# Attention ahead of two layers of experts: scores and exponentials issued by head, with the two row halves out of step

## The chip, the cores and the metric

One core of one Trainium2 chip runs the whole program in one launch. The metric is the device time of that launch in microseconds (us); lower is better. The engines are named as in the profile: PE (TensorE matmul) with PEld (its weight loads), DVE (VectorE), ACT (ScalarE), POOL (GpSimd), SP (SyncE, which here only issues DMAs).

## The reference

Three stages follow one another in float32: attention with pooled queries, a mixture of 4 experts for every token, and a mixture of 8 experts with one expert per token. The change touches the first stage and where it hands over to the second.

```python
batch, n_heads, seq, head_dim = 2, 8, 1152, 64
q_pool = q.reshape(B, H, S // 2, 2, D).mean(axis=3)             # 576 query rows
scores = scale * np.matmul(q_pool, k.transpose(0, 1, 3, 2))     # 576 x 1152
scores = scores - np.max(scores, axis=-1, keepdims=True)
attn = np.exp(scores)
attn = attn / (np.sum(attn, axis=-1, keepdims=True) + 1e-09)
attn_out = np.matmul(attn, v)
# x: attn_out as 1152 x 512; then
# moe1: out += p[:, e] * (relu(x @ w1[e]) @ w2[e]) for 4 experts, 512 -> 1024 -> 512
# moe2: the same with 8 experts, of which each row takes one
```

## The kernel before

The 16 (batch, head) combinations go through in 8 pairs of heads. The first head of a pair lies on partitions 0 to 63, the second on 64 to 127, so that a matmul of one head uses one half of TensorE's rows and the two heads' matmuls can run side by side. A pair has two jobs, g = 2p with 256 query rows and g = 2p + 1 with 320, and a job has 9 chunks of 128 keys. A job is issued in two halves: the first takes chunks 0 to 3, the second chunks 4 to 8. Scores are kept transposed, keys on partitions and query rows along the free axis.

For one chunk, `score` (L105 to L113) issues four matmuls for each head into one PSUM tile S of two banks: high part of q with high and low part of k, low part of q with high part of k, and a row of ones with the negated row maximum, mr. One ACT instruction (L113) then takes the exponential of both heads, 128 x 512 or 128 x 640, into a tile E. There are two S tiles, so the scores of chunk c + 2 wait until the exponential of chunk c has read its tile. POOL adds the E tiles of a job up (`add`, L120), eight additions a job. PE multiplies E by v into O (`av`, L126) and sums the added tile over the keys with a matrix of ones (`total`, L132). ACT copies the sums (L134) and O (L138), DVE takes reciprocals (L140), POOL multiplies (L142), ACT casts the high part of x and POOL takes the low part (L149, L150). The last job differs: `ndir` gives it four chunks that PE sums itself (eight matmuls with ones) in place of POOL.

The row maxima of the next job are made among the scores of this one: `smax` (L80 to L86) issues one 384-key matmul for each head and DVE reduces each; the last 64 rows of both heads go together in `tmax` (L90, L91). `mT` (L101 to L104) turns the maxima into mr. The first half of a shorter job also transposes q of the next pair (L69), the last half of a longer job k of the pair after that (L58), with ACT making the high parts and DVE the low parts. The order of the instructions on each engine is the order in which this code is written out by hand, since the scheduler is off for the stretch.

After attention, weights go in 128 x 1024 pieces through a staging tile `st` (DMA on SP, L204), a cast to the high part on ACT (L212) and a subtraction for the low part on DVE (L215), into a tile w of a ring. Staging and ring are allocated in the room that attention's pools leave when they close. The pool `ld`, which holds the k and q as loaded, lies on the right side, and `kq`, which holds their parts, on the left; the first four ring tiles thus lie under `ld`, which is free once the last pair has been transposed, and the first four splits stand inside the last pairs.

Loads of the first pair are issued on SP (k) and on ACT's queue (q), those of the second pair on ACT's queue (L39 to L42), all later ones on SP.

Of the kernel before, what the change touches and what calls it, by code (L numbers as in the profile page):

```python
# [9 lines left out]
def attention(tc, q, k, v, xT, identF, NJ=16):  # L10

    nc=tc.nc
    B,H,S,D=q.shape
    Q=S//2; NC=S//128; NP=NJ//2; NG=2*NP; C1=4
    DI=0
    RB=(0,); RA=(1,2)
    JOB=((0,256),(256,320))
    HD=(slice(0,64),slice(64,128))
    with ExitStack() as ctx:
        def pool(name,bufs,**kw): return ctx.enter_context(tc.tile_pool(name=name,bufs=bufs,**kw))  # L20
        ld=pool("ld",2,side="right")
        one=pool("one",1); vp=pool("vp",3); ep=pool("ep",10); es=pool("es",2); fp=pool("fp",3); sm=pool("sm",3); kq=pool("kq",2)
# [9 lines left out]
        def load(p):  # L32
            b,h0=divmod(2*p,H)
            kn=ld.tile([128,NC,2,D],F32,name="kn"); qn=ld.tile([128,2,5,2,D],F32,name="qn"); vn=vp.tile([128,2,NC,D],F32,name="vn")
            st['ld',p]=kn,qn; st['v',p]=vn
            ek,eq=(nc.sync,nc.scalar) if p==0 else (nc.scalar,nc.scalar) if p==1 else (nc.sync,nc.sync)
            ks=[slice(0,3),slice(3,6),slice(6,9)] if p==0 else [slice(0,9)]
            for n in range(2):
                eq.dma_start(qn[:,n,0:4],q[b,h0+n,0:1024].rearrange("(i p r) d -> p i r d",p=128,r=2))  # L39
                eq.dma_start(qn[:,n,4],q[b,h0+n,896:1152].rearrange("(p r) d -> p r d",r=2))  # L40
            for c in ks:
                for n in range(2): ek.dma_start(kn[:,c,n],k[b,h0+n].rearrange("(p c) d -> p c d",c=NC)[:,c])  # L42
            if p>1: load_v(p)
# [9 lines left out]
        def kT(p,g):  # L53
            if g==0: st['k',p]=[kq.tile([128,S],F32R,name=n) for n in ("kh","kl")]
            kn=st['ld',p][0]; kh,kl=st['k',p]
            f=T1(384) if g<2 or p==0 else psS.tile([128,2,512],F32,name="S")[:,0,0:384]
            cs=slice(g*384,(g+1)*384)
            for m in range(3): nc.tensor.transpose(f[:,m*128:(m+1)*128],kn[:,3*g+m].rearrange("p h d -> p (h d)"),identF)  # L58
            nc.scalar.copy(kh[:,cs],f)
            lo=lambda: nc.vector.tensor_tensor(out=kl[:,cs],in0=f,in1=kh[:,cs].bitcast(F32),op=ALU.subtract)  # L60
            if p==0: st['lo',g]=lo
            else: lo()
        def qT(p):
            st['q',p]=[kq.tile([128,Q],F32R,name=n) for n in ("qh","ql")]
            qs=st['qs',p]; qh,ql=st['q',p]
            if p==0: s0=psS.tile([128,2,512],F32,name="S")
            for mm,o,cs in ((range(4),0,slice(0,512)),((4,),64,slice(512,576))):
                f=T1(512) if p else (s0[:,0] if o==0 else s0[:,1])
                for i,m in enumerate(mm): nc.tensor.transpose(f[:,i*128:(i+1)*128],qs[:,m].rearrange("p h d -> p (h d)"),identF)  # L69
                src=f[:,o:o+cs.stop-cs.start]  # L70
                nc.scalar.activation(out=qh[:,cs],in_=src,func=AF.Copy,scale=0.0625)
                nc.vector.scalar_tensor_tensor(out=ql[:,cs],in0=src,scalar=0.0625,in1=qh[:,cs].bitcast(F32),op0=ALU.mult,op1=ALU.subtract)
            for h in range(2): nc.gpsimd.tensor_copy(qt[p%2][HD[h],HD[h]],qh[HD[h],512:576])
# [3 lines left out]
        def smax(g,i,early=False):  # L77

            p,u=divmod(g,2); c,t=divmod(i,2); m=m3(g); kh=st['k',p][0]; qh=st['q',p][0]
            if early: ss=psS.tile([128,2,512],F32,name="S")[:,:,0:384].rearrange("p h n -> h p n")  # L80
            else: ss=[T1(384) for h in range(2)]
            for h in range(2):
                nc.tensor.matmul(ss[h],qh[HD[h],(2*u+t)*128:(2*u+t+1)*128],kh[HD[h],c*384:(c+1)*384],start=True,stop=True)  # L83
            if early: nc.vector.tensor_reduce(out=m[:,t,:,c],in_=ss.rearrange("h p n -> p h n"),axis=AX.X,op=ALU.max)
            else:
                for h in range(2): nc.vector.tensor_reduce(out=m[:,t,h,c:c+1],in_=ss[h],axis=AX.X,op=ALU.max)  # L86
# [18 lines left out]
        def score(g,c):  # L105
            p,u=divmod(g,2); o,n=JOB[u]
            kh,kl=st['k',p]; qh,ql=st['q',p]; mr=st['m',g]
            s=psS.tile([128,2,512],F32,name="S"); cs=slice(c*128,(c+1)*128); os=slice(o,o+n)
            ops=((kh[:,cs],qh[:,os]),(kl[:,cs],qh[:,os]),(kh[:,cs],ql[:,os]),(ones,mr))
            for i,(l,r) in enumerate(ops):  # L110
                for h in range(2): nc.tensor.matmul(s[:,h,0:n],l[HD[h]],r[HD[h]],start=i==0,stop=i==3)  # L111
            E=ep.tile([128,2,320],F32,name="E"); st['E',g,c]=E
            nc.scalar.activation(out=E[:,:,0:n],in_=s[:,:,0:n],func=AF.Exp)  # L113
        def ndir(g): return 4 if g==NG-1 else DI
# [38 lines left out]
        with tc.manual_schedule():  # L153
            qsum(0)
            for n in range(3): kT(0,n)
            qT(0)
            load_v(0)
            for i in range(6): smax(0,i,True)
            neg(0); st['lo',0](); mT(0); st['lo',1](); st['lo',2]()
            load(1); load_v(1)  # L160
            for h in range(4*NP):
# [7 lines left out]
                for i,c in enumerate(range(C1) if first else range(C1,NC)):  # L169
                    if rl and i in RB: smax(*rl.pop(0))  # L170
                    score(g,c)
                    add(g,c)
                    if rl and i in RA: smax(*rl.pop(0))
                    if h==0:
                        for _ in range(2):
                            if rl: smax(*rl.pop(0))
                    if first and c==2 and g>1: fin(g-2)
# [606 lines left out]
```

## Time and profile before

| | us |
|---|---|
| runs shown | 818.16 to 824.17, median 822.31 of 3 |
| the profiled execution | 819.94, of which the span is 818.1 |
| attention ends, experts begin | 257.21 |
| PE busy | 783.2 (96%) |
| DVE / ACT / POOL busy | 374.1 / 300.9 / 278.1 |

The profile follows one execution. Its span runs from the first to the last instruction; the device time holds 1.8 us more. In the 40 slices of the page POOL stands at 9 for slices 4 to 12, the slices of attention, PE at 9 nearly everywhere, and the granted TensorE clock at 9 of 10 or more in every slice. Times of rows are us from the span's start; in the trace's names S is the score tile, T a shared PSUM tile, m and M the maxima, es the sum of exponentials.

### The profile page before, as it was taken

The page shows a single profiled execution, that of the slowest core. Times are in us where ns is not written, and L with a number is a line of the kernel's source. Part 1 is how long each engine was busy: PE and PEld are TensorE (multiplying, and loading weights), DVE is VectorE, ACT ScalarE, POOL GpSimd, SP SyncE. Part 2 cuts the span into 40 slices and gives each one's busy share as a digit, 9 for nine tenths or more (in the row PEclk, how much of TensorE's full clock was granted, in tenths as well). Part 3 has the DMA queues.
Part 4 walks back from the last instruction along what each step waited for, and adds up shares of the span by engine and source line. Part 5 has one row for each costly group of instructions (what it writes and reads, how often), then busy time and mean ns, then how long its engine had stood idle before and what let it go on. Part 6 is the DMA issues. An engine that isn't in the chain of part 4 may idle for free. (4 is left out here: it accounts for less than half of the span.)

```text
span 818.1 us, 13046 instructions
## 1 busy us (share of the span) xinstructions
PE 783.2 (96%) x5128; PEld 641.0 (78%) x5128; DVE 374.1 (46%) x789; ACT 300.9 (37%) x557; POOL 278.1 (34%) x256
## 2 busy tenths in 40 slices
PE   4999999998999999999999999999999999998996
PEld 2667677666667998998989989889898888877673
DVE  4676867777836110431214412144253589563510
ACT  1356555556546121330103301033141455471611
POOL 1689999999994000000000000000000242442301
PEclk9999999999999999999999999999999999999998
DMA  8703311301206000140003100000053141996981
GB/s 280 180 2 91 91 53 40 91 31 32 74 1 229 6 1 1 61 145 1 1 1 102 54 0 1 1 1 1 26 183 153 40 168 46 339 333 234 335 295 70
DMA packets 57735, 77.53 MB, mean 95 GB/s; under 512 B 23031, under 2 KB 33271, under 8 KB 57664
## 3 DMA queue, kind: packets, MB, share of 16 engines
q1 hardware_dynamic: 50752, 69.12, 25.3%
q0 software_dynamic: 1600, 4.98, 1.8%
q10 hardware_dynamic: 5312, 2.49, 1.2%
q8 instruction: 43, 0.70, 0.4%
q14 instruction: 28, 0.23, 0.1%
HBM read 71.86 MB, written 4.98 MB: 94 GB/s over the span
## 5 line engine op out<-in xcount | busy, mean ns | idle before, releaser
L120 POOL TENSOR_TENSOR es<-es,E 128x512 f32<-128x512 f32 (+1 forms) x108 | 154.3, 1429 | 7.7 <-ACT E L113 0.9
L375 POOL TENSOR_TENSOR r_n<-r_ss,half 128x1 f32<-128x1 f32 x9 | 5.8, 649 | 372.7 <-ACT X L374 372.6
L245 PE MATMUL ps<-xb,w 128*128 128x384 f32 x384 | 129.4, 337 | 0.0
L243 PE MATMUL ps<-xb,w 128*128 128x384 f32 x384 | 129.3, 337 | 0.0
L248 DVE SCALAR_TENSOR_TENSOR hl<-ps,hh 128x384 fp32r<-128x384 f32 x96 | 53.4, 557 | 150.3 <-ACT hh L247 150.1
L247 ACT ACTIVATE hh<-ps 128x384 fp32r<-128x384 f32 x96 | 47.2, 491 | 201.0 <-PE ps L245 201.0
L113 ACT ACTIVATE E<-S 128x512 f32<-128x512 f32 (+1 forms) x144 | 90.0, 650 | 72.8 <-PE S L111 65.6
L258 PE MATMUL py<-w,hl 128*128 128x512 f32 x288 | 113.4, 394 | 0.0
L257 PE MATMUL py<-w,hh 128*128 128x512 f32 x288 | 113.1, 393 | 0.0
L256 PE MATMUL py<-w,hh 128*128 128x512 f32 x288 | 112.5, 391 | 0.0
L86 DVE TENSOR_REDUCE m<-T 128x1 f32<-128x384 f32 x180 | 91.5, 552 | 32.1 <-PE T L83 29.3
L244 PE MATMUL ps<-xc,w 128*128 128x384 f32 x288 | 97.0, 337 | 0.0
L215 DVE TENSOR_TENSOR w<-st,w 128x1024 fp32r<-128x1024 f32 x53 | 74.5, 1419 | 42.4 <-ACT w L212 41.1
L126 PE MATMUL O<-E,vn 128*64 128x320 f32 (+1 forms) x576 | 76.9, 411 | 0.0
L212 ACT CAST w<-st 128x1024 fp32r<-128x1024 f32 x60 | 61.8, 1054 | 36.2 <-PE py L258 23.9
L243 PEld LDWEIGHTS ps<-xb,w 128*128 128x128 f32 x384 | 72.1, 188 | 0.9 <-issue 0.5
L245 PEld LDWEIGHTS ps<-xb,w 128*128 128x128 f32 x384 | 72.1, 188 | 0.0
L257 PEld LDWEIGHTS py<-w,hh 128*128 128x128 f32 x288 | 54.1, 188 | 11.7
L256 PEld LDWEIGHTS py<-w,hh 128*128 128x128 f32 x288 | 54.1, 188 | 11.3
L258 PEld LDWEIGHTS py<-w,hl 128*128 128x128 f32 x288 | 54.1, 188 | 10.9
L262 DVE SCALAR_TENSOR_TENSOR y<-py,p,y 128x512 f32<-128x512 f32 x27 | 20.2, 750 | 90.6 <-PE py L258 90.6
L126 PEld LDWEIGHTS O<-E,vn 128*64 128x64 f32 x576 | 38.6, 136 | 28.1 <-issue 5.5
(369 smaller groups left out, 1342.4 us busy)
## 6 DMA issues: line engine op xcount, KB each, us to landing
st<-in_moe_w SPq DMA_DIRECT2D x104, 512.0 KB, 5.5
vn<-in_v SPq DMA_DIRECT2D x14, 288.0 KB, 3.4
kn<-in_k SPq DMA_DIRECT2D x12, 288.0 KB
qn<-in_q SPq DMA_DIRECT2D x12, 256.0 KB, 4.2
ysc<-y SPq DMA_DIRECT2D x9, 256.0 KB, 2.0
qn<-in_q ACTq DMA_DIRECT2D x4, 256.0 KB, 3.8
qn<-in_q SPq DMA_DIRECT2D x12, 64.0 KB, 3.7
kn<-in_k SPq DMA_DIRECT2D x6, 96.0 KB, 3.6
```

The costliest lines, as they stand in the source:

```text
L86: for h in range(2): nc.vector.tensor_reduce(out=m[:,t,h,c:c+1],in_=ss[h],axis=AX.X,op=ALU.max)
L113: nc.scalar.activation(out=E[:,:,0:n],in_=s[:,:,0:n],func=AF.Exp)
L120: nc.gpsimd.tensor_tensor(out=s,in0=st['E',g,0][:,:,0:n] if c==1 else s,in1=st['E',g,c][:,:,0:n],op=ALU.add)
L126: for h in range(2): nc.tensor.matmul(O[HD[h],0:n],vn[:,h,c],st['E',g,c][:,h,0:n],start=c==0,stop=c==NC-1)
L212: if he=='A': nc.scalar.copy(wh,st)
L215: (nc.vector if le=='V' else nc.gpsimd).tensor_tensor(out=wl,in0=st,in1=wh.bitcast(F32),op=ALU.subtract)
L243: nc.tensor.matmul(ps,wh[:,fs],xh[dc],start=(dc==0),stop=False)
L244: nc.tensor.matmul(ps,wh[:,fs],xl[dc],start=False,stop=False)
L245: nc.tensor.matmul(ps,wl[:,fs],xh[dc],start=False,stop=(dc==3))
L256: nc.tensor.matmul(py,hh[:,us],wh[:,cs],start=(fc==0),stop=False)
L257: nc.tensor.matmul(py,hh[:,us],wl[:,cs],start=False,stop=False)
L258: nc.tensor.matmul(py,hl[:,us],wh[:,cs],start=False,stop=(fc==7))
```

## The change

Each head gets its own score tiles, S0 and S1, of one bank each (two of each), and its own exponentials of 256 or 320 columns. `streams` lists the score matmuls and the row maxima of each head by a pattern (S a chunk's scores, m a row maximum), gives each a nominal start, and issues the two heads' lists merged by that; the row maxima of the two heads stand at different places of the patterns. `add` is called when a chunk's second exponential has been issued. In the longer jobs PE sums the last chunk in place of POOL (`ndir`). The small casts of q for the wide maximum move from POOL to ACT. For the first pair, ACT copies the transposed q and k out of PSUM and POOL takes the low parts, where DVE read PSUM. The loads of the second pair are issued on SP right behind the first pair's, and the first maxima stand between the transposes. `ld` and `kq` change sides, so the first ring tiles lie under the parts of k and q, which are read until the last score.

```diff
-    DI=0
-    RB=(0,); RA=(1,2)
+    PAT=(("SSmSmSm","mSSmSmS"),("SSmSmSmS","mSSmSmSS"),("SmmSmmSmmS","SmmSmmSmmS"))
...
-        ld=pool("ld",2,side="right")
-        one=pool("one",1); vp=pool("vp",3); ep=pool("ep",10); es=pool("es",2); fp=pool("fp",3); sm=pool("sm",3); kq=pool("kq",2)
+        ld=pool("ld",2)
+        one=pool("one",1); vp=pool("vp",3); ep=pool("ep",10); es=pool("es",2); fp=pool("fp",3); sm=pool("sm",3); kq=pool("kq",2,side="right")
...
-            ek,eq=(nc.sync,nc.scalar) if p==0 else (nc.scalar,nc.scalar) if p==1 else (nc.sync,nc.sync)
+            ek,eq=(nc.sync,nc.scalar) if p==0 else (nc.sync,nc.sync)
...
-            lo=lambda: nc.vector.tensor_tensor(out=kl[:,cs],in0=f,in1=kh[:,cs].bitcast(F32),op=ALU.subtract)
-            if p==0: st['lo',g]=lo
-            else: lo()
+            if p==0:
+                w=ep.tile([128,2,320],F32,name="E").rearrange("p h n -> p (h n)")[:,0:384]
+                def low():
+                    nc.scalar.copy(w,f)
+                    nc.gpsimd.tensor_tensor(out=kl[:,cs],in0=w,in1=kh[:,cs].bitcast(F32),op=ALU.subtract)
+                st['low',g]=low
+            else: nc.vector.tensor_tensor(out=kl[:,cs],in0=f,in1=kh[:,cs].bitcast(F32),op=ALU.subtract)
...
-            for h in range(2): nc.gpsimd.tensor_copy(qt[p%2][HD[h],HD[h]],qh[HD[h],512:576])
+                if p:
+                    nc.vector.scalar_tensor_tensor(out=ql[:,cs],in0=src,scalar=0.0625,in1=qh[:,cs].bitcast(F32),op0=ALU.mult,op1=ALU.subtract)
+                else:
+                    w=ep.tile([128,2,320],F32,name="E").rearrange("p h n -> p (h n)")[:,0:cs.stop-cs.start]
+                    nc.scalar.activation(out=w,in_=src,func=AF.Copy,scale=0.0625)
+                    nc.gpsimd.tensor_tensor(out=ql[:,cs],in0=w,in1=qh[:,cs].bitcast(F32),op=ALU.subtract)
+            for h in range(2): nc.scalar.copy(qt[p%2][HD[h],HD[h]],qh[HD[h],512:576])
...
+        def smax1(g,i,h,early=False):
+            p,u=divmod(g,2); c,t=divmod(i,2); m=m3(g); kh=st['k',p][0]; qh=st['q',p][0]
+            s=psS.tile([128,512],F32,name=f"S{h}")[:,0:384] if early else T1(384)
+            nc.tensor.matmul(s,qh[HD[h],(2*u+t)*128:(2*u+t+1)*128],kh[HD[h],c*384:(c+1)*384],start=True,stop=True)
+            nc.vector.tensor_reduce(out=m[:,t,h,c:c+1],in_=s,axis=AX.X,op=ALU.max)
         def smax(g,i,early=False):
-            p,u=divmod(g,2); c,t=divmod(i,2); m=m3(g); kh=st['k',p][0]; qh=st['q',p][0]
-            if early: ss=psS.tile([128,2,512],F32,name="S")[:,:,0:384].rearrange("p h n -> h p n")
-            else: ss=[T1(384) for h in range(2)]
-            for h in range(2):
-                nc.tensor.matmul(ss[h],qh[HD[h],(2*u+t)*128:(2*u+t+1)*128],kh[HD[h],c*384:(c+1)*384],start=True,stop=True)
-            if early: nc.vector.tensor_reduce(out=m[:,t,:,c],in_=ss.rearrange("h p n -> p h n"),axis=AX.X,op=ALU.max)
-            else:
-                for h in range(2): nc.vector.tensor_reduce(out=m[:,t,h,c:c+1],in_=ss[h],axis=AX.X,op=ALU.max)
+            for h in range(2): smax1(g,i,h,early)
...
-        def score(g,c):
-            p,u=divmod(g,2); o,n=JOB[u]
-            kh,kl=st['k',p]; qh,ql=st['q',p]; mr=st['m',g]
-            s=psS.tile([128,2,512],F32,name="S"); cs=slice(c*128,(c+1)*128); os=slice(o,o+n)
-            ops=((kh[:,cs],qh[:,os]),(kl[:,cs],qh[:,os]),(kh[:,cs],ql[:,os]),(ones,mr))
-            for i,(l,r) in enumerate(ops):
-                for h in range(2): nc.tensor.matmul(s[:,h,0:n],l[HD[h]],r[HD[h]],start=i==0,stop=i==3)
-            E=ep.tile([128,2,320],F32,name="E"); st['E',g,c]=E
-            nc.scalar.activation(out=E[:,:,0:n],in_=s[:,:,0:n],func=AF.Exp)
-        def ndir(g): return 4 if g==NG-1 else DI
+        def score(g,c,h,i):
+            p,u=divmod(g,2); o,n=JOB[u]; hd=HD[h]
+            kh,kl=st['k',p]; qh,ql=st['q',p]; cs=slice(c*128,(c+1)*128); os=slice(o,o+n)
+            if i==0: st['s',h]=psS.tile([128,512],F32,name=f"S{h}")[:,0:n]
+            s=st['s',h]
+            l,r=((kh[:,cs],qh[:,os]),(kl[:,cs],qh[:,os]),(kh[:,cs],ql[:,os]),(ones,st['m',g]))[i]
+            nc.tensor.matmul(s,l[hd],r[hd],start=i==0,stop=i==3)
+            if i<3: return
+            if ('E',g,c) not in st: st['E',g,c]=ep.tile([128,2,320],F32,name="E"); st['n',g,c]=0
+            nc.scalar.activation(out=st['E',g,c][:,h,0:n],in_=s,func=AF.Exp)
+            st['n',g,c]+=1
+            if st['n',g,c]==2: add(g,c)
+        def streams(g,cs,ms,pat,between):
+            n=JOB[g%2][1]; L=[]
+            for h in range(2):
+                t=0; ci=iter(cs); mi=iter(ms)
+                for x in pat[h]:
+                    if x=='S':
+                        c=next(ci,None)
+                        if c is None: continue
+                        for i in range(4): L.append((t,h,lambda c=c,h=h,i=i: score(g,c,h,i),(c,h,i))); t+=9+.425*n
+                    else:
+                        m=next(mi,None)
+                        if m is None: continue
+                        L.append((t,h,lambda m=m,h=h: smax1(*m,h),None)); t+=172
+            for t,h,f,k in sorted(L,key=lambda z: z[:2]):
+                f()
+                if k: between(*k)
+        def ndir(g): return 4 if g==NG-1 else g%2
...
-            for n in range(3): kT(0,n)
-            qT(0)
+            load(1)
+            kT(0,0); kT(0,1); st['low',0](); qT(0)
+            smax(0,0,True); smax(0,1,True); st['low',1]()
+            kT(0,2); st['low',2]()
+            for i in range(2,6): smax(0,i,True)
             load_v(0)
-            for i in range(6): smax(0,i,True)
-            neg(0); st['lo',0](); mT(0); st['lo',1](); st['lo',2]()
-            load(1); load_v(1)
+            neg(0); mT(0)
+            load_v(1)
...
-                for i,c in enumerate(range(C1) if first else range(C1,NC)):
-                    if rl and i in RB: smax(*rl.pop(0))
-                    score(g,c)
-                    add(g,c)
-                    if rl and i in RA: smax(*rl.pop(0))
-                    if h==0:
-                        for _ in range(2):
-                            if rl: smax(*rl.pop(0))
-                    if first and c==2 and g>1: fin(g-2)
+                def between(c,hh,i):
+                    if hh==1 and i==3 and first and c==2 and g>1: fin(g-2)
+                streams(g,range(C1) if first else range(C1,NC),rl,PAT[h==0 and 2 or (not first)],between)
```

The first place is ACT at the start of the program; qh, kh are high parts, vn, kn, qn loads, E stands in for a scratch copy where it is written from T. Before:

```order
L59 CAST kh<-T 128x384 x3
L71 ACTIVATE qh<-S 128x512
L71 ACTIVATE qh<-S 128x64
L46 DMA vn<-in_v 128x576 x2
L102 CAST mr_222<-T 128x256
L39 DMA qn<-in_q 128x4x128
L40 DMA qn<-in_q 128x128
L39 DMA qn<-in_q 128x4x128
L40 DMA qn<-in_q 128x128
L42 DMA kn<-in_k 128x9x64 x2
L113 ACTIVATE E<-S 128x2x256 x4
```

And with the change:

```order
L58 CAST kh<-T 128x384 x2
L62 COPY E<-T 128x384
L73 ACTIVATE qh<-T 128x512
L78 ACTIVATE E<-T 128x512
L73 ACTIVATE qh<-T 128x64
L78 ACTIVATE E<-T 128x64
L80 COPY qt_138<-qh 64x64 x2
L62 COPY E<-T 128x384
L45 DMA vn<-in_v 128x576 x2
L107 CAST mr_256<-T 128x256
L120 ACTIVATE E<-S_266 128x256
L120 ACTIVATE E<-S_268 128x256
```

The six loads of the second pair have left the place ahead of the first exponential; copies out of PSUM and the two small casts have come in ahead of mr. (One cast and one copy more, of the last third of k, stand ahead of the loads of v.)

The second place is PE in the first half of the shorter job of a late pair; S_2614 and S_2628 are score tiles of the first head, S_2620 and S_2633 of the second, L83 and L88 row maxima. Before:

```order
L83 MATMUL T<-kh,qh 128x384 x2
L111 MATMUL S<-qh,kh 128x256 x2
L111 MATMUL S<-qh,kl 128x256 x2
L111 MATMUL S<-ql,kh 128x256 x2
L111 MATMUL S<-mr_2796,ones 128x256 x2
```

And with the change:

```order
L117 MATMUL S_2614<-qh,kh 128x256
L88 MATMUL T<-kh,qh 128x384
L117 MATMUL S_2614<-qh,kl 128x256
L117 MATMUL S_2620<-qh,kh 128x256
L117 MATMUL S_2614<-ql,kh 128x256
L117 MATMUL S_2620<-qh,kl 128x256
L117 MATMUL S_2614<-mr_2574,ones 128x256
L117 MATMUL S_2620<-ql,kh 128x256
L117 MATMUL S_2628<-qh,kh 128x256
L117 MATMUL S_2620<-mr_2574,ones 128x256
```

Where both heads took the same step together, the first head begins with scores while the second has its row maximum, and the second head follows one step behind; their tiles are filled, and released to the exponentials, one after the other.

The third place is DVE at the end of attention. Before, four low parts of weights (L215) stand among the maxima of the last pairs, of which this is the first piece:

```order
L86 TENSOR_REDUCE m_2610<-T 128x1 x2
L215 TENSOR_TENSOR w<-st,w 128x1024
L86 TENSOR_REDUCE m_2610<-T 128x1 x2
L215 TENSOR_TENSOR w<-st,w 128x1024
L86 TENSOR_REDUCE m_2610<-T 128x1 x2
L215 TENSOR_TENSOR w<-st,w 128x1024
```

With the change the first low parts (L237) stand at the last reciprocals:

```order
L166 RECIPROCAL r<-r 128x128 x2
L237 TENSOR_TENSOR w<-st,w 128x1024 x2
L166 RECIPROCAL r<-r 128x160 x2
L341 TENSOR_SCALAR enT<-X,rt_3920 128x32
L168 TENSOR_TENSOR x<-x,r 128x320
L366 MEMSET base 128x8
L237 TENSOR_TENSOR w<-st,w 128x1024 x2
L176 TENSOR_TENSOR xc_96<-x,xb_95 128x320
```

None is left among the maxima; two go ahead of the last job's reciprocals and two behind its product.

## Rows read from the trace of the kernel before

**Rows 1.** Windows: stretch, length, busy of PE PEld DVE ACT POOL, clock, DMA.

```profile
118.87:147.09 28.22, 27.67 (x273) 19.78 (x272) 20.15 (x39) 16.33 (x35) 27.22 (x25) 1.00 0.26 67
...
175.41:206.80 31.39, 28.40 (x272) 20.00 (x273) 25.20 (x43) 19.87 (x39) 30.39 (x26) 1.00 0.18 55
206.80:233.51 26.71, 25.91 (x257) 18.17 (x256) 18.75 (x35) 14.12 (x29) 25.79 (x23) 1.00 0.11 40
233.51:257.21 23.70, 22.39 (x213) 14.79 (x211) 7.24 (x7) 14.61 (x28) 19.29 (x17) 1.00 0.26 85
```

**Rows 2.** Timeline of POOL: start, duration, engine, line, operation, out<-in, count.

```profile
115.28 1.27 POOL L120 TENSOR_TENSOR es<-E 128x512 f32<-128x512 f32 x1
...
119.79 0.52 POOL L73 CAST qt<-qh 64x64 fp32r<-64x64 f32 x2
...
133.66 9.76 POOL L120 TENSOR_TENSOR es<-es,E 128x640 f32<-128x640 f32 x6
...
144.04 1.29 POOL L120 TENSOR_TENSOR es<-E 128x512 f32<-128x512 f32 x1
```

**Rows 3.** Timeline of PE in a second half of the shorter job.

```profile
118.87 0.28 PE L111 MATMUL S<-qh,kh 64*128 64x256 f32 x2
...
119.34 0.28 PE L111 MATMUL S<-qh,kh 64*128 64x256 f32 x2
...
120.83 0.41 PE L83 MATMUL T<-kh,qh 64*128 64x384 f32 x2
121.00 0.35 PE L111 MATMUL S<-qh,kh 64*128 64x256 f32 x2
...
121.74 0.39 PE L111 MATMUL S<-qh,kh 64*128 64x256 f32 x2
```

**Rows 4.** Groups by shape, ACT, 33.77 to 233.51: busy, mean ns | idle, releasers.

```profile
L113 ACT ACTIVATE E<-S 128x640 f32<-128x640 f32 x63 | 42.9, 704 | 31.0 <-PE S L111 30.1 <-POOL es L120 0.5
L113 ACT ACTIVATE E<-S 128x512 f32<-128x512 f32 x63 | 36.0, 598 | 30.4 <-PE S L111 29.9
```

**Rows 5.** Timeline of ACT: two exponentials in a row.

```profile
113.01 1.09 ACT L113 ACTIVATE E<-S 128x512 f32<-128x512 f32 x2 [2.92 <-PE S L111]
```

**Rows 6.** Waits, 33.77 to 233.51: who waits for what, us in total, times, longest.

```profile
PEld S L111 <- ACT E L113: 16.0, 41, 1.1
...
ACT xb L149 <- POOL x L142: 11.0, 10, 2.4
```

**Rows 7.** Timeline of PE in the last halves.

```profile
247.04 0.41 PE L111 MATMUL S<-qh,kh 64*128 64x320 f32 x2 [0.27 <-ACT E L113]
...
248.75 0.41 PE L111 MATMUL S<-qh,kh 64*128 64x320 f32 x2 [0.27 <-ACT E L113]
...
252.27 2.32 PE L132 MATMUL T<-E,ones 128*64 128x320 f32 x16
```

**Rows 8.** Timeline of DVE in the pair of 31.39 us.

```profile
201.20 1.64 DVE L215 TENSOR_TENSOR w<-st,w 128x1024 fp32r<-128x1024 f32 x1
```

**Rows 9.** Timeline of PE where the heads once ran half a chunk apart.

```profile
206.93 0.28 PE L111 MATMUL S<-qh,kh 64*128 64x256 f32 x1
207.04 0.28 PE L111 MATMUL S<-ql,kh 64*128 64x256 f32 x1
207.05 0.28 PE L111 MATMUL S<-qh,kl 64*128 64x256 f32 x1
```

**Rows 10.** Timeline of ACT and DVE in the first pair.

```profile
25.79 1.09 ACT L113 ACTIVATE E<-S 128x512 f32<-128x512 f32 x2 [5.83 <-DMA qn<-in_q]
...
29.17 1.49 DVE L91 TENSOR_REDUCE m<-T 128x1 f32<-128x384 f32 x3 [2.46 <-PE T L90]
```

**Rows 11.** Timeline of DVE and PE at the hand-over to the experts.

```profile
256.60 1.23 DVE L215 TENSOR_TENSOR w<-st,w 128x1024 fp32r<-128x1024 f32 x1 [1.21 <-ACT w L212]
...
257.74 2.16 DVE L140 RECIPROCAL r<-r 128x160 f32<-128x160 f32 x2
...
264.68 0.41 PE L318 MATMUL X<-identF,en 8*128 8x8 f32 x4 [0.78 <-DVE en L315]
```

More of the change, by code (lines that the diff above doesn't have):

```diff
@@ L55, in kT @@
             kn=st['ld',p][0]; kh,kl=st['k',p]
-            f=T1(384) if g<2 or p==0 else psS.tile([128,2,512],F32,name="S")[:,0,0:384]
+            f=T1(384) if g<2 or p==0 else psS.tile([128,512],F32,name="S0")[:,0:384]
             cs=slice(g*384,(g+1)*384)
@@ L59, in kT @@
             nc.scalar.copy(kh[:,cs],f)
-            lo=lambda: nc.vector.tensor_tensor(out=kl[:,cs],in0=f,in1=kh[:,cs].bitcast(F32),op=ALU.subtract)
-            if p==0: st['lo',g]=lo
-            else: lo()
+            if p==0:
[5 more added lines that the diff above has]
+            else: nc.vector.tensor_tensor(out=kl[:,cs],in0=f,in1=kh[:,cs].bitcast(F32),op=ALU.subtract)
         def qT(p):
             st['q',p]=[kq.tile([128,Q],F32R,name=n) for n in ("qh","ql")]
-            qs=st['qs',p]; qh,ql=st['q',p]
-            if p==0: s0=psS.tile([128,2,512],F32,name="S")
+            qs=st['qs',p]; qh,ql=st['q',p]; ff=[]
             for mm,o,cs in ((range(4),0,slice(0,512)),((4,),64,slice(512,576))):
-                f=T1(512) if p else (s0[:,0] if o==0 else s0[:,1])
+                f=T1(512); ff.append((f[:,o:o+cs.stop-cs.start],cs))
                 for i,m in enumerate(mm): nc.tensor.transpose(f[:,i*128:(i+1)*128],qs[:,m].rearrange("p h d -> p (h d)"),identF)
-                src=f[:,o:o+cs.stop-cs.start]
+            for src,cs in ff:
                 nc.scalar.activation(out=qh[:,cs],in_=src,func=AF.Copy,scale=0.0625)
-                nc.vector.scalar_tensor_tensor(out=ql[:,cs],in0=src,scalar=0.0625,in1=qh[:,cs].bitcast(F32),op0=ALU.mult,op1=ALU.subtract)
-            for h in range(2): nc.gpsimd.tensor_copy(qt[p%2][HD[h],HD[h]],qh[HD[h],512:576])
+                if p:
[5 more added lines that the diff above has]
+            for h in range(2): nc.scalar.copy(qt[p%2][HD[h],HD[h]],qh[HD[h],512:576])
         def m3(g):
```

## The prediction

> **What bounds the kernel now.** The windows come first [rows 1]. Attention ends at 257.21 us; the experts follow. The change edits attention and, of the experts, only the start, so everything behind that is taken to shift unchanged. Within attention a pair of heads takes 28.22 us in the steady middle; PE is busy for 27.67 of it, POOL for 27.22 and ACT for 16.33. Both PE and POOL look full, so the next question is which one the other waits for.
>
> POOL's timeline [rows 2] shows additions back to back. From a pair's first addition to the next pair's is 144.04 - 115.28 = 28.76 us, a little more than PE's pitch: POOL falls behind slowly and would soon be the pace. PE's timeline [rows 3] shows that PE is not full of work. Two chunks start 0.47 apart when nothing holds them, and a pair of row maxima takes 121.00 - 120.83 = 0.17. The five chunks of this half start within 121.74 - 118.87 = 2.87 us, while the work between those starts is 4 x 0.47 + 2 x 0.17 = 2.22: 0.65 us are waits that the modelled matmul ends hide. The four halves of a pair, counted alike, give about 2.0 us (the waits of [rows 6], 16.0 in seven pairs, come to 2.3 each). The waits name the cause [rows 6]: a score weight load stood 41 times, 16.0 us in seven pairs, behind an exponential that had not yet emptied its PSUM tile. So it is the round trip score, exponential, next score that costs, with two tiles to alternate; ACT as a whole is far from full.
>
> **The change, part by part**, against the profiled execution's own 819.94 us. The median of the runs is 822.31, 2.4 higher; I add that at the end.
>
> *Exponentials by head.* ACT takes 0.598 for 512 columns and 0.704 for 640 [rows 4]: 0.83 ns a column and about 0.17 fixed. The second of two in a row adds only 1.09 - 0.60 = 0.49 [rows 5], so about 0.11 of the fixed part hides. By these rows 256 columns cost 0.385 alone and 0.28 in a row, 320 columns 0.44 and 0.33. Two heads need 0.56 or 0.66 of ACT per chunk against 0.47 (0.59 in the longer job) plus maxima on PE. What a score waits for is the exponential of its own head, 0.21 shorter than the joint one, and the heads' halves are moved apart so that ACT takes them in turn. PE's cycle of two chunks, 1.38 to 1.66 us by the starts in [rows 3], gets some 0.2 shorter, and the work in it is 1.1. Of the 2.0 us about 1.35 should go. The rest, 0.65, stays: about 0.15 because ACT's 0.56 exceeds PE's 0.47 where no maximum lies between, and about 0.5 for two low-part casts on ACT, which wait 11.0 us over seven pairs for POOL's product [rows 6] with exponentials queued behind them. Bounds: all 2.0 goes, or nothing.
>
> The Trainium skill, "ScalarE: Activation LUTs", section "What ACT_TABLE_LOAD costs", prices an ACTIVATE with immediate operands at 186 ns plus 0.833 ns a column, with about 93 ns hidden back to back. Here [rows 4] show 0.17 for its fixed part and [rows 5] 0.11 for what hides. By the page, an estimate, a chunk takes ACT 0.61 and 0.72 instead of 0.56 and 0.66; if half of that extra were bare, some 0.5 us a pair, the time would come out 3 to 4 us later. The rows of this case are taken.
>
> *Row maxima and scores in streams.* The number of matmuls is the same; only their order changes. That two row halves run side by side although half a chunk apart is seen once in this trace [rows 9]: one head's third score matmul starts at 207.04 between the other head's first and second, at 206.93 and 207.05, which keep the usual step of 0.12 (a quarter of 0.47). So the new order is costed at nothing, covered by that concurrency; what it costs if that fails is the slower rival below.
>
> *Sum of the last chunk on PE in the longer jobs.* Four rows more on PE per pair: 2.32 for 16 [rows 7] is 0.145 each, so +0.55 (0.58 by that row, 0.5 if the other row half hides some). POOL loses one 640-column addition, 9.76 / 6 = 1.63, and its two casts of 0.52, which go to ACT [rows 2]: its pair becomes 28.76 - 1.63 - 0.52 = 26.6.
>
> *A pair* is then 28.22 - 1.35 + 0.55 = 27.4 on PE, above POOL's 26.6, which stops being the pace. Of the seven pairs from 33.77 to 233.51, six take 27.4 and the last, which has no successor to prepare, 26.71 - 0.8 = 25.9: 190.3 against 199.74, **-9.4**. About 4.0 of that is the pair of 31.39 [rows 1]. There the first weight splits ran on ACT and DVE within the scores, beside POOL's additions, and a low part took 1.64 [rows 8] where one takes 1.23 at 256.60 [rows 11]. With the weights under k and q these splits can only come after the last score, so the pair becomes a normal one.
>
> *The last three halves*, 233.51 to 257.21, have no maxima to cover waits. Two chunks take 248.75 - 247.04 = 1.71 [rows 7] for 1.18 of work, five such waits in all: 2.65. ACT's 0.66 and 0.56 leave 14 chunks with 0.07 to 0.09 each, 1.0. **-1.6** (bounds 0 and -2.6).
>
> *The start.* The first exponential waited 5.83 us behind loads of the second pair that stand on ACT's queue [rows 10]; those are now on SP, issued at the top. The scores could run at about 20 us. The next limit is DVE: 12 maxima and 3 wide ones at 1.49 / 3 = 0.5 are 7.4 us and end near 27.3, where they end at 30.66 now. With the same tail the pairs start 3.3 earlier: **-3.3**. Bounds -1 (the k and q casts of the second pair, or the added ACT copies of the first, are late) and -5 (all that the wait was).
>
> *The hand-over.* Four splits, formerly inside the pairs, now stand between the last exponential and the experts, 1.23 each on DVE [rows 11]. Two low parts go ahead of the last reciprocals there, two behind the product that follows them. The sums end near 255 [rows 7], the reciprocals (2.16) at 257.5 or so, the product must wait for the copy of O after PE's last matmul at 257.2, so I estimate the third low part at 260.5 and the fourth at 261.8 on the present clock. PE, from 257.2 on with three groups in turn at some 0.17 a matmul, comes to them about 0.1 and 0.4 us earlier. The loads that follow wait for those tiles and are wanted some 10 us later: hidden. Against this stands the 0.78 that PE now waits for the router's embedding at 264.68, and which moves. Net **+0.5**; bounds -0.8 (nothing waits) and +3 (two splits and their casts bare).
>
> Sum: -3.3 - 9.4 - 1.6 + 0.5 = -13.8, so 806.1 for a profiled execution and **808.5** for the median.
>
> **Rivals.**
> - *All stalls go and POOL paces.* At 26.6 the seven pairs take 6 x 26.5 + 25 = 184, 6 less than above: 802. For it: POOL is nearly full now. Against: ACT's casts still wait for POOL. Chance 0.17.
> - *The small exponentials don't overlap.* At 0.77 and 0.88 a chunk, 1.54 and 1.76 for two, PE's cycle is what it is now: stalls stay at 2.0, the sums add 0.55, a pair is 28.8. Pairs: 6 x 28.8 + 27.3 = 200.1, +0.4; the start -3.3 and the hand-over +0.5 remain: -2.4, so 820. For it: twice as many instructions and semaphores on ACT. Against: [rows 5] show the overlap at 512 columns. Chance 0.20.
> - *Single maxima run in single file (slower).* Now the two heads' maxima share 0.17. If out of step each of the 24 per pair holds the array alone, that is 12 x 0.17 = 2.0 us more a pair, 14 in all: 823. If the score matmul beside each loses its cover too, 24 x 0.12 = 2.9 us a pair more come on top, 20 in all: 843. Middle 832; it decides from about 1.4 us a pair, where it eats the gain in the stalls. Against: [rows 9]. Chance 0.06. The Trainium skill, "TensorE: Matmul & The Clock Gate", Part 3, says that matmuls end strictly in the order of issue; by it a score issued behind a wider maximum could not end before it, a milder form of this rival.
> - *The hand-over is bare.* The low parts or the second layer's weights come 3 to 4 us late: 813. For it: DVE has four low parts and the reciprocals in one queue. Chance 0.04. What is left, 0.53, is the forecast, with a range of its own of 804 to 814 from the bounds of the start, the stalls and the hand-over.
>
> **How the numbers follow.** About 1%, 8 us, can be told from no change. Faster by that is below 814: all of POOL's rival, the hand-over's, most of the forecast, but not all of it, since half the stall kept would add 5 to 7: 0.66. Within 1%, 814 to 830: the rival of the exponentials, the upper end of the forecast and half of the single file: 0.28. Slower: 0.06, the single file at its dearer half and what I have not seen. The range runs from POOL's rival, 801, to the exponentials', 821.
>
> **What the profile after would show.** Pairs 27.4 apart in the windows, POOL busy for less than 26.6 of them; PE's weight loads waiting for exponentials a third of 16.0 us; 256-column exponentials in rows of two at 0.28 each; the first pair's chunk 4 near 30.4; no pair of 31; at the hand-over low parts behind the reciprocals with a PE wait under 1 us. Wrong: exponentials over 0.38 in a stream with ACT nowhere idle in a half, or score matmuls 0.17 and more apart around a maximum, or POOL without a gap while PE waits for it.

## The result and the profile after

The changed kernel takes 816.17 us (811.94 to 817.17, 13 runs) against 822.07 for the kernel before: a ratio of 0.991 with a 95% interval from 0.989 to 0.993, 5.9 us faster. That lies in the range, 7.7 us above the forecast of 808.5. The profiled execution took 811.94, the lowest of the 13, with a span of 810.1.

Windows of the changed kernel, columns as in [rows 1]; the first three answer to its pairs:

```profile
114.14:142.08 27.94, 27.92 (x276) 20.74 (x274) 19.83 (x39) 17.89 (x54) 25.86 (x23) 1.00 0.26 67
...
170.01:198.36 28.35, 28.21 (x276) 20.74 (x274) 20.47 (x43) 18.54 (x56) 26.14 (x23) 1.00 0.20 64
198.36:224.50 26.14, 26.14 (x262) 19.22 (x261) 17.52 (x34) 15.56 (x47) 23.66 (x20) 1.00 0.16 58
224.50:248.58 24.08, 24.02 (x217) 16.08 (x215) 8.04 (x8) 15.80 (x42) 16.22 (x15) 1.00 0.14 44
248.58:810.10 561.52, 550.70 (x2950) 477.03 (x2948) 204.03 (x468) 165.07 (x281) 58.07 (x48) 0.99 0.29 105
```

A steady pair takes 27.94 instead of 28.22, not 27.4; the pair of 31.39 is 28.35; the last halves take 24.08 where they took 23.70. PE is busy throughout, POOL for 25.86 of 27.94. Part by part, us against the profiled execution before:

| part | forecast | measured |
|---|---|---|
| start (33.77 before, 30.29 after) | -3.3 | -3.5 |
| seven pairs (199.74, 194.2) | -9.4 | -5.5 |
| last three halves (23.70, 24.08) | -1.6 | +0.4 |
| experts, from their first matmul | +0.5 | +0.6 here, +5.5 in a second profile |

The start is taken where the first pair's later scores run on without a break; their first matmul already stands at 29.64, and counted from there the start gained 4.1 and the seven pairs 4.9.

The last row needs the experiments: a second profile of the same kernel, of a run near the median, has experts of 566.42 us. From the experts' first matmul on the two profiles run alike for 478 us. Then one stretch of the second layer takes 25.43 us in the first and 30.02 in the second, where PE waits 2.58 us for DVE and the clock granted over the stretch falls to 0.94:

```profile
726.17:751.60 25.43, 24.63 (x172) 19.38 (x169) 9.62 (x14) 10.46 (x19) 8.40 (x4) 1.00 0.85 323
```

```profile
726.58:756.60 30.02, 26.19 (x171) 20.54 (x169) 12.68 (x14) 10.56 (x19) 7.70 (x4) 0.94 0.70 268
738.30 0.38 PE L585 MATMUL ps<-y,w 128*128 128x256 f32 x1 [2.58 <-DVE hl L589]
```

All other profiles of this document, that of the kernel before included, have 28.3 us or more there. The +0.6 of the first profile, so near the forecast, is thus an accident of one execution.

POOL's timeline, against [rows 2]: five additions of a longer job in a row instead of six, 1.62 each.

```profile
109.19 1.28 POOL L146 TENSOR_TENSOR es<-E 128x512 f32<-128x512 f32 x1 [0.86 <-ACT E L120]
...
127.34 8.10 POOL L146 TENSOR_TENSOR es<-es,E 128x640 f32<-128x640 f32 x5
```

The exponentials by shape over the seven pairs, as in [rows 4], and two in a row in the first pair, as in [rows 5]:

```profile
L120 ACT ACTIVATE E<-S 128x320 f32<-128x320 f32 x126 | 46.8, 439 | 21.4 <-PE S L117 19.7 <-POOL es L146 0.4 <-PE T L88 0.2
L120 ACT ACTIVATE E<-S 128x256 f32<-128x256 f32 x126 | 40.1, 386 | 22.0 <-PE S L117 19.3
```

```profile
18.79 0.66 ACT L120 ACTIVATE E<-S 128x256 f32<-128x256 f32 x2 [0.78 <-PE S L117]
```

0.386 alone and 0.66 - 0.38 = 0.28 behind another, the two prices of the forecast. (An estimate from the figures of the Trainium skill, "ScalarE: Activation LUTs", section "What ACT_TABLE_LOAD costs", is 0.306 for the second, 0.03 more than measured here.)

PE at a row maximum, for the slower rival, against [rows 9]:

```profile
115.14 0.28 PE L117 MATMUL S<-ql,kh 64*128 64x256 f32 x1
115.20 0.33 PE L88 MATMUL T<-kh,qh 64*128 64x384 f32 x1
115.26 0.27 PE L117 MATMUL S<-mr,ones 64*128 64x256 f32 x1
```

One head's maximum starts between two score matmuls of the other, which keep their 0.12: no single file.

The waits from 29.64 to 224.5, against [rows 6]: by this view no weight load stands behind an exponential any more, the casts no longer stand behind POOL's product, and a new wait has come, of the wide maxima on DVE. But 9.0 us of the score weight loads' waits have no cause that the view names, and 3.4 stand behind ACT's copy of O, so it can't be read from here whether the waits on exponentials fell to a third of 16.0.

```profile
PEld S L117 <- issue: 9.0, 22, 0.5
...
PEld S L117 <- ACT x L164: 3.4, 7, 0.5
...
PEld T L95 <- DVE m L89: 2.4, 12, 0.2
```

### The profile page after: what moved, and what is told of

It is laid out like the page before. It is cut to its first block, busy times and chain, and to the rows that moved or that the text cites. A ratio compares the mean times of both kernels' runs of the same rounds, so it can differ in the third digit from the quotient of the medians.

```text
span 810.1 us, 13178 instructions
## 1 busy us (share of the span) xinstructions
PE 789.5 (97%) x5156; PEld 651.6 (80%) x5156; DVE 364.6 (45%) x790; ACT 314.9 (39%) x722; POOL 264.3 (33%) x238
## 5 line engine op out<-in xcount | busy, mean ns | idle before, releaser
L146 POOL TENSOR_TENSOR es<-es,E 128x512 f32<-128x512 f32 (+1 forms) x101 | 141.5, 1401 | 14.0 <-ACT E L120 8.0
L120 ACT ACTIVATE E<-S 128x320 f32<-128x320 f32 (+1 forms) x288 | 99.2, 413 | 52.9 <-PE S L117 48.5
L278 PE MATMUL py<-w,hh 128*128 128x512 f32 x288 | 114.6, 398 | 0.0
L279 PE MATMUL py<-w,hh 128*128 128x512 f32 x288 | 114.4, 397 | 0.0
L89 DVE TENSOR_REDUCE m<-T 128x1 f32<-128x384 f32 x180 | 89.1, 551 | 46.6 <-PE T L88 36.8
L237 DVE TENSOR_TENSOR w<-st,w 128x1024 fp32r<-128x1024 f32 x53 | 71.5, 1368 | 44.7 <-ACT w L234 44.4
L117 PE MATMUL S<-qh,kh 64*128 64x320 f32 (+1 forms) x288 | 80.9, 336 | 0.1
L117 PE MATMUL S<-qh,kl 64*128 64x320 f32 (+1 forms) x288 | 74.0, 302 | 0.0
L117 PE MATMUL S<-ql,kh 64*128 64x320 f32 (+1 forms) x288 | 72.5, 299 | 0.0
L117 PE MATMUL S<-mr,ones 64*128 64x320 f32 (+1 forms) x288 | 71.1, 294 | 0.0
```

Source lines behind the costliest of these rows:

```text
L89: nc.vector.tensor_reduce(out=m[:,t,h,c:c+1],in_=s,axis=AX.X,op=ALU.max)
L117: nc.tensor.matmul(s,l[hd],r[hd],start=i==0,stop=i==3)
L120: nc.scalar.activation(out=st['E',g,c][:,h,0:n],in_=s,func=AF.Exp)
L146: nc.gpsimd.tensor_tensor(out=s,in0=st['E',g,0][:,:,0:n] if c==1 else s,in1=st['E',g,c][:,:,0:n],op=ALU.add)
L237: (nc.vector if le=='V' else nc.gpsimd).tensor_tensor(out=wl,in0=st,in1=wh.bitcast(F32),op=ALU.subtract)
L278: nc.tensor.matmul(py,hh[:,us],wh[:,cs],start=(fc==0),stop=False)
```

## Experiments

Names: the last halves are the three without row maxima; a score stretch is the time from a half's first score or maximum to PE's first other instruction. The theory after the profile was that what is left of the stalls is still the round trip of score, exponential and next score, with two tiles a head and both heads in PE's one queue.

**More tiles in the last halves.** A T tile takes the third chunk's scores.

```diff
-            if i==0: st['s',h]=psS.tile([128,512],F32,name=f"S{h}")[:,0:n]
+            if i==0: st['s',h]=T1(n) if st['few'] and c in (2,6) else psS.tile([128,512],F32,name=f"S{h}")[:,0:n]
...
-            n=JOB[g%2][1]; L=[]
+            n=JOB[g%2][1]; L=[]; st['few']=not ms
```

> The changed kernel, but in the three halves without row maxima (after 224.5 us) the third chunk's scores of each head go to one of the three T tiles, which are idle there, so no score waits for an exponential two chunks back. Theory (round trip: score, exponential, next score, with two tiles a head and both heads in one queue of PE): the score stretches 3.64, 3.15 and 4.17 us become about 3.1, 2.6 and 3.5, the stretch from 224.5 to the experts 22.3 instead of 24.08, the total 1.5 to 2 us lower. Rival A (ACT's rate: ten exponentials take 3.3 us whatever the tiles): stretches lose 0.2 at most each, total 0 to -0.5. Rival B (matmuls of heads apart run slower on the array): no change.

808.24 us, 0.982 of the kernel before (0.980 to 0.985). Its window of the last halves:

```profile
224.47:246.10 21.63, 21.63 (x218) 15.24 (x216) 9.05 (x8) 15.11 (x42) 17.27 (x15) 1.00 0.13 35
```

24.08 becomes 21.63; the score stretches 3.64, 3.15, 4.17 become 2.76, 2.54, 3.21, more than the theory had put. The round trip is shown, ACT's rate and the array are out. The total fell by 7.9, more than these 2.5 us; the rest comes below.

Why the change itself gained nothing there is in its PE timeline. The two heads are apart only by a row maximum, and without maxima they are issued in step:

```profile
225.43 0.28 PE L117 MATMUL S<-mr,ones 64*128 64x256 f32 x2
225.77 0.66 PE L117 MATMUL S<-qh,kh 64*128 64x256 f32 x2
226.05 0.50 PE L117 MATMUL S<-qh,kl 64*128 64x256 f32 x2
```

The two `qh,kh` are spread over 0.66: the first head's starts at 225.77, when its exponential has ended, the second's 0.28 later, when its own has, and the first head's next matmul stands behind that in the queue until 226.05. The second head sets the pace, and its exponential ends 0.66 after the first began; the joint one ended after 0.60.

**Heads in step in the pairs too.**

```diff
-    PAT=(("SSmSmSm","mSSmSmS"),("SSmSmSmS","mSSmSmSS"),("SmmSmmSmmS","SmmSmmSmmS"))
+    PAT=(("mSSmSmS","mSSmSmS"),("mSSmSmSS","mSSmSmSS"),("SmmSmmSmmS","SmmSmmSmmS"))
```

> The changed kernel with the same pattern for both heads, so row maxima and scores of both heads stand side by side again, while exponentials stay by head. Theory (what was gained in the pairs comes from the offset; with both heads in step the second exponential of a chunk ends 0.66 us after the first begins, later than the joint one did): the four score stretches of a pair, 13.6 us now and 14.7 before the change, return to 14.5 to 15, a pair to about 28.9, the total 7 us up, about 823. Rival (the shorter exponentials bring the gain, the order does not matter): stretches within 0.3 of 13.6, total within 2 us.

819.34 us, 0.994 (0.992 to 0.996). A pair:

```profile
117.39:145.93 28.54, 28.54 (x276) 20.89 (x276) 19.95 (x39) 17.83 (x55) 25.90 (x23) 1.00 0.26 66
```

The four stretches sum to 14.5 (14.7 before the change, 13.6 in it), and the pair is 0.6 longer than in the changed kernel: the gain comes from the offset, 0.9 in the stretches; shorter exponentials alone bring 0.2. The other 0.3 are given back behind the scores, most of it because the two wide maxima take 0.54 here and 0.78 in the changed kernel, which the next experiment is about. The total is 3 us above the changed kernel's, not 7, since a pair came out at 28.5 and not 28.9.

**Wide maxima later.** In the longer job's first half `tmax` moves behind `av`.

```diff
-                if h%4==2 and p+1<NP: tmax(p+1,0); tmax(p+1,1)
...
-                        av(g-1,5,NC); norm(g-1,0); total(g-1)
+                        av(g-1,5,NC); norm(g-1,0)
+                        if h%4==2 and p+1<NP: tmax(p+1,0); tmax(p+1,1)
+                        total(g-1)
```

> The changed kernel, with the two wide maxima of the longer job's first half issued behind the multiplication by v instead of ahead of it. Theory (the row maxima now come later in the half, so the second wide one waits for DVE to empty a T tile, 0.78 us for two instead of 0.55): the two take 0.55 again, a pair 27.7 instead of 27.93, the total about 1.6 lower. Rival (the 0.23 belong to the end of the out-of-step scores, not to DVE): they stay or turn up at the next maxima; total unchanged.

814.43 us, 0.990 (0.988 to 0.991). In the changed kernel the two wide maxima take 0.78 up to the next instruction, 0.55 before; the maxima of the heads now come one by one, and DVE is behind:

```profile
123.78 0.85 PE L95 MATMUL T<-kh,qt 128*128 128x384 f32 x2
124.56 1.95 PE L152 MATMUL O<-E,vn 128*64 128x256 f32 x16
```

```profile
122.18 2.42 DVE L89 TENSOR_REDUCE m<-T 128x1 f32<-128x384 f32 x5 [0.61 <-PE S L117]
```

Moved, they take 0.55 again, but the multiplication and the sum take 0.15 more, and a pair is 27.85 (112.11 to 139.96), only 0.09 less. The wait on DVE is real; undone this way it is worth 0.6 us in all, not 1.6. That attention ends 2.3 us earlier in this profile (246.32 against 248.58) is mostly something else: the first pair's matmuls of 256 columns take 0.28 from 24.3 us on, where the changed kernel's still take 0.41 at 25.3, and its later scores begin at 27.97 instead of 29.64, ahead of any place that the edit touches. The lower total is therefore no measure of the edit.

**All additions on POOL.** `ndir` gives 0 for all jobs but the last.

> The changed kernel with all eight additions of the longer jobs on POOL again. Theory (PE is the pace, POOL just below): PE loses 0.54 us a pair, POOL goes from 25.9 to about 27.5 us of work a pair and becomes the pace with its gaps: pair 27.5 to 27.9 instead of 27.93, total 0 to 3 us lower. Rival A (PE alone is the pace): pair 27.4, total 4.3 lower. Rival B (POOL at 27.5 plus its waits for exponentials is well above PE): pair 28.3 or more, total 3 us up.

819.41 us, 0.996 (0.992 to 0.999). Two windows, a steady pair and the sixth; then POOL, DVE and PE in the sixth:

```profile
84.69:112.08 27.39, 27.37 (x272) 20.41 (x271) 19.82 (x39) 17.91 (x55) 26.53 (x22) 1.00 0.27 69
...
167.44:203.68 36.24, 30.54 (x273) 22.12 (x272) 22.73 (x45) 19.79 (x61) 31.10 (x28) 0.91 0.19 60
```

```profile
187.02 6.42 POOL L146 TENSOR_TENSOR es<-es,E 128x640 f32<-128x640 f32 x4
...
193.40 0.57 POOL L333 TENSOR_TENSOR n<-n,half 8x1 f32<-8x1 f32 x1
...
194.01 0.14 DVE L334 TENSOR_SCALAR n<-n 8x1 f32<-8x1 f32 x1 [3.71 <-POOL n L333]
...
196.70 0.68 PE L88 MATMUL T<-kh,qh 64*128 64x384 f32 x1 [5.17 <-DVE m L89]
```

Rival A is right for a pair, 27.39: PE alone paces, and the four rows with ones cost their 0.54. The total is 3 us worse, as rival B had it, but not by its mechanism, and for a reason that I had missed. Since the pools changed sides, the router's embedding no longer comes at the hand-over but within the sixth pair. One instruction of it stands in POOL's queue behind the additions, DVE waits for it, and the row maxima stand behind that on DVE. Here POOL is late, and PE loses 5.17 us and, behind that wait, for a while its higher clock (granted 0.91 over the window). In the changed kernel POOL is less late and this costs 0.42 (a score stretch of 3.38 instead of 2.96), most of the pair's 28.35 against 27.94.

**Pools back on their old sides.** `ld` to the right, `kq` to the left.

> The changed kernel with the loaded k and q on the right side again and their parts on the left, so that the first four weights are loaded early and split within the last pairs, and the router's embedding comes at the hand-over again. Theory (the splits were what made the pair of 31.39 long): the pair that held 28.35 goes to 30 to 31.5, the hand-over gains about 0.5, the total 2 us up. Rival (that pair was long because POOL was behind, which it no longer is): 28.5 to 29, total within 1 us.

815.30 us, 0.992 (0.988 to 0.995).

```profile
170.46:200.35 29.89, 28.33 (x276) 20.77 (x274) 24.34 (x43) 21.65 (x58) 26.97 (x22) 1.00 0.21 61
```

The pair with the splits grows to 29.89, attention to 250.25 (248.58): the splits cost 1.5 us, not the 3.2 by which that pair stood above its neighbours. The rest may be POOL's lag at that time; no run separates it. Of the other differences 0.5 is a later start of the pairs (30.11 for 29.64), which the edit does not touch. The total came out 0.9 below the changed kernel's and not 2 above, because the experts' 512-column matmuls ran faster in this program (229.0 ns for 233.3, see the experts' step).

**Second loads late again.** `load(1)` back behind the first maxima, on ACT's queue.

> The changed kernel with the loads of the second pair back on ACT's queue behind the row maxima of the first. Theory (the first exponentials waited behind those loads): the first pair's chunk 4 starts at 33 to 34 instead of 29.6, total 3.5 us up. Rival (the start was gained by the low parts on POOL and the earlier maxima): within 1 us.

817.03 us, 0.995 (0.993 to 0.997). ACT and DVE in the first pair, as in [rows 10]:

```profile
22.08 1.21 ACT L120 ACTIVATE E<-S 128x256 f32<-128x256 f32 x4 [4.04 <-DMA qn<-in_q]
...
26.96 1.49 DVE L96 TENSOR_REDUCE m<-T 128x1 f32<-128x384 f32 x3 [0.85 <-PE T L95]
```

The exponentials wait 4.04 us for the loads again, but chunk 4 starts at 30.75 instead of 29.64 and runs on at 31.30 instead of 30.29, only 1.0 to 1.1 later, where the theory had 3.5. Kernels of this document whose start is that of the changed kernel have their chunk 4 anywhere from 27.97 to 30.68, so even this 1.0 may not be the loads'. My reason for the start is refuted: the exponentials were late, but not what held the pairs.

**The experts' step.** The kernel with more tiles had gained 5 us that attention does not show. In the steady middle of the first experts layer PE never waits, and a third of an expert (96 matmuls of 384 columns, 72 of 512) takes, in the kernel before and in the changed one:

```profile
325.04:358.17 33.13, 33.13 (x170) 30.17 (x169) 11.55 (x15) 12.95 (x18) 0.00 (x0) 1.00 0.19 65
```

```profile
316.19:349.94 33.75, 33.75 (x170) 30.56 (x168) 11.57 (x15) 12.94 (x18) 0.00 (x0) 1.00 0.19 63
```

The granted clock is 1.00 in both. The step, from one matmul's start to the next one's, is on average 173.4 and 228.9 ns before, 176.7 and 233.3 after, all through some 320 us. The kernel with more tiles has 173.4 and 228.9. First the changed kernel itself again:

> The changed kernel itself once more, on the same chip as the other runs of this group. If the slower steps of the experts' matmuls (176.7 and 233.3 ns) belong to the program, they are there again and attention ends at 248.6 again; if they belong to the execution, 173.4 and 228.9 can appear, and the total then lies 4 to 7 us lower than with the slow ones.

816.48 us (812.04 to 817.52), 0.993 (0.990 to 0.996), the same steps; the experts whole:

```profile
248.88:815.30 566.42, 552.58 (x2950) 478.22 (x2948) 207.32 (x468) 165.79 (x281) 56.99 (x48) 0.99 0.29 104
```

So the steps went with the program, in both of its profiles. Then one instruction more on PE between attention and the experts, in the changed kernel, in it twice, and in the kernel before:

```diff
             total(g); av(g,5,NC); fin(g-1)
+            for _ in range(1): nc.tensor.transpose(T1(128),identF,identF)
```

> The changed kernel with one 128 x 128 transpose more on PE between attention and the experts, into a T tile that nobody reads. Theory (the step of the experts' matmuls, 173 or 177 and 229 or 233 ns, is set by how PE enters a stretch that it then runs through without a wait, not by what the stretch does): in some of the kernels with a small shift at that place the steps change; here 176.7 and 233.3 become 173.3 or 229 in at least one of the two shapes, and the total falls 2 to 6 us. Rival (the steps belong to the placement of tiles or loads in the changed kernel): 176.7 and 233.3 as before, total up 0.1.

> The same with two transposes more. Theory: the steps may again be either; that they differ between this kernel, the one with one transpose and the changed kernel would speak for the entry. Rival: 176.7 and 233.3 in all three.

> The kernel before with one transpose more at the same place. Its own steps were 173.4 and 228.9. Theory: they can change to 176.7 or 233.3 here, total up to 5 us more; if they stay, the kernel before is no witness against it, since two of four outcomes are fast. Rival (placement): they stay.

810.01 us (0.986, 0.984 to 0.988), 811.89 (0.989, 0.987 to 0.991) and 827.93 (1.008, 1.005 to 1.010). The steps are 173.4 and 228.9 with one and with two transposes more, and 176.7 and 233.3 in the kernel before with one. Windows of the first and of the third:

```profile
315.03:348.15 33.12, 33.12 (x169) 30.16 (x168) 11.54 (x15) 12.94 (x18) 0.00 (x0) 1.00 0.19 66
247.99:808.20 560.21, 546.93 (x2953) 474.88 (x2953) 207.55 (x468) 165.72 (x281) 56.98 (x48) 0.99 0.29 105
```

```profile
328.48:362.23 33.75, 33.75 (x169) 30.57 (x168) 11.56 (x15) 12.94 (x18) 0.00 (x0) 1.00 0.19 65
259.64:826.60 566.96, 552.83 (x2953) 478.44 (x2953) 204.52 (x469) 162.32 (x279) 59.03 (x51) 0.99 0.28 98
```

One transpose of about 0.1 us makes the changed kernel's experts 6 us shorter and those of the kernel before 6 us longer, with the same matmuls on the same tiles. The rival (placement) is out. The transpose is not the only difference, though: with it the four transposes of the router's embedding stand behind the experts' first matmul instead of ahead of it, and a few matmuls of the first third change places; from the second third on the order is the same. The order alone does not select the step either, since the kernel with more tiles has the changed kernel's order there and the faster steps. With the faster steps in both, the change is worth 11 us (810.01 against 821.02, 0.986), with the slower ones in both 11.5 (816.48 against 827.93), not 6.

**Both edits, and both with one transpose more.**

> The changed kernel with both edits: T tiles for the third chunk in the last three halves, and the wide maxima behind the multiplication by v. Theory: the first took 2.5 us off the last three halves, the second 0.09 off each of seven pairs (less than I expected), so attention ends 3.1 us earlier than in the changed kernel. The rest of the 8 us by which the first alone was faster than the changed kernel's median lay in the experts, whose matmuls ran at 173.4 and 228.9 ns a step there and at 176.7 and 233.3 in the profile of the changed kernel. If these steps go with the program, this one has its own; if with the execution, any. Total 805 to 812.

> The version with T tiles in the last halves and the late wide maxima, with one transpose more between attention and the experts. Its steps were 176.7 and 229. Theory: with the entry the steps may become 173.4 and 229, then 805; or stay, then 808; or both slow, then 811.

808.17 us, 0.983 (0.980 to 0.986), with steps of 176.7 and 229.0, and 807.73 us, 0.982 (0.979 to 0.984), with 173.4 and 228.9, for which 805 had been expected. These and the kernel with more tiles alone beat both kernels; among the three the runs tell no difference.

## Why the prediction was right, and where it was not

It held by direction and by the whole range, 801 to 821, which reaches from a clear gain almost to none. The forecast's own range, 804 to 814, missed, and the outcome that came, within 1%, had a chance of 0.28 against 0.66 for a larger gain. The second profile, of 817.21 us, lies some 11 above the 806.1 that I put for a profiled execution: about 6 of them in attention, which I put to end at 242.9 and which ended at 248.88, and 5 in the experts, nearly all by the step of their matmuls. Of the rivals, the exponentials overlap as costed, the heads' matmuls do not run in single file, POOL is not the pace of a steady pair, and nothing is bare at the hand-over. The steps, one by one:

- **Exponentials by head: the mechanism right, 1.35 was 1.1.** The prices 0.28 and 0.33 are there, the wait of exponentials on POOL's product is gone, the offset carries the gain (heads in step: 0.6 back). I had not priced that both heads share one queue, so that the later head's wait holds the earlier one.
- **Row maxima costed at nothing: wrong by 0.23 a pair.** They overlap on PE, as said, but come later, and the wide maxima behind them wait for DVE. With the 0.25 above this is the step from 27.4 to 27.94, some 3.4 of the 3.9 us missing in the pairs; the embedding in the sixth pair is the other 0.4.
- **The last three halves, -1.6: wrong.** I took the offset to hold there; it comes from the maxima alone, and there are none. Their score stretches sum to 10.96 against 10.92 before, no gain at all; 0.34 of the +0.4 in the table are the embedding's four transposes, which now stand ahead of the experts' first matmul. With more tiles the stalls go, by 2.5 us.
- **The sum on PE: right**, 0.54 for 0.55; POOL below PE: right, and it is needed, for POOL late is what cost 36.24 us in one pair.
- **The splits: half right.** They cost 1.5 us of the 3.2 that I gave them.
- **The start: the size right, -3.5, the reason not.** With the loads back on ACT it keeps all but about 1.0. What holds the earlier start is the rest: the first maxima begin at 10.86 on DVE where they began at 12.69, and the first half's new order keeps DVE in work; these two were not separated.
- **The hand-over, +0.5: wrong, to the good side.** DVE's timeline has the low parts behind the reciprocals, but they end at 250.77 and 251.91, before PE needs them; PE's first matmuls start no more than 0.28 apart, and the 0.78 for the embedding is gone:

```profile
246.84 2.17 DVE L166 RECIPROCAL r<-r 128x160 f32<-128x160 f32 x2 [2.13 <-ACT r L160]
...
249.56 1.21 DVE L237 TENSOR_TENSOR w<-st,w 128x1024 fp32r<-128x1024 f32 x1
...
250.69 1.22 DVE L237 TENSOR_TENSOR w<-st,w 128x1024 fp32r<-128x1024 f32 x1
```

Counted from the end of attention's own matmuls, the first third takes 1.57 us more than the next one before, and 0.43 now, so the hand-over gained 1.1. First and second third, before and with the change:

```profile
257.21:291.91 34.70, 33.92 (x174) 30.62 (x173) 11.60 (x26) 8.73 (x18) 2.04 (x3) 1.00 0.25 81
291.91:325.04 33.13, 33.13 (x170) 30.16 (x168) 4.46 (x8) 6.00 (x11) 0.00 (x0) 1.00 0.00 1
```

```profile
248.24:282.43 34.19, 34.19 (x174) 30.99 (x173) 14.70 (x25) 11.74 (x18) 0.00 (x0) 1.00 0.50 172
282.43:316.19 33.76, 33.76 (x170) 30.57 (x169) 4.46 (x8) 5.99 (x11) 0.00 (x0) 1.00 0.00 0
```

- **"Everything behind that is taken to shift unchanged": the costliest failure, some 6 us.** Eight of the experts' 12 thirds run without a break and take 33.75 instead of 33.13, 5.0 us; with the rest, and with what the hand-over gave back, the experts as a whole grew by 5.5 (566.42 against 818.1 - 257.21). In the first profile the faster stretch of the second layer hides most of it. What selects the step is not known, so this could not have been forecast from the rows at hand.

## What to carry to other kernels

An offset between two streams in one queue pays only as far as the later stream's wait does not stand in front of the earlier one; look at the places where the offset's cause is absent, and add buffers there first. A gain or loss of under 1% in one stage of a kernel that is bound by matmuls says little until the step of the matmuls elsewhere has been compared: put the starts of the same block side by side in both traces. Two profiles of one kernel should be at hand before a difference is split into parts; here the first was the lowest of 13 runs, and differed from the second by 4.6 us in a stretch that the change does not touch. When pools move, look for other work that moves with them, and in whose queue it then stands.

## What the runs showed of the hardware

A long stretch of matmuls without waits ran at one of two steps, 173.4 or 176.7 ns for 384 columns and 228.9 or 233.3 for 512, at a granted clock of 1.00, for some 320 us; the step was the same in two profiles of one program and changed with one transpose ahead of the stretch, in both directions. In three programs (wide maxima later, both edits, pools on old sides) the 384-column matmuls took the slower and the 512-column ones the faster step. Programs with the same order of matmuls from the experts' first one on differ in it. What selects it is open.
